# Attention steps issued singly and in 64-column pieces, turning joined with later scores, and a plan that counts instruction blocks

## The chip, the cores and the metric

The kernel runs on one core of one Trainium2 chip. The metric is the device time of one execution in microseconds, lower is better. Three runs of the kernel before took 547.86, 543.38 and 552.81 us; their median, 547.86 us, is the time before. The tensor engine is called PE here, its weight loads PEld, the vector engine DVE, the scalar engine ACT, GpSimd POOL and the engine that issues the transfers SP.

## What is computed

A recurrent attention (mLSTM) over 4 batches, 8 heads, 768 positions and head size 40, followed by a feed-forward part of 320 to 2048 to 320 on the 3072 tokens that come out. All in float32.

```python
for t in range(S):
    m_new = np.maximum(f_gate[:, :, t] + m, i_gate[:, :, t])
    f_stab = np.exp(f_gate[:, :, t] + m - m_new)
    i_stab = np.exp(i_gate[:, :, t] - m_new)
    m = m_new
    C = f_stab[..., None, None] * C + i_stab[..., None, None] * np.einsum('bhd,bhe->bhde', vt, kt)
    n = f_stab[:, :, None] * n + i_stab[:, :, None] * kt
    h_tilde = np.einsum('bhde,bhe->bhd', C, qt)
    denom = np.maximum(np.abs(np.einsum('bhd,bhd->bh', n, qt)[:, :, None]), 1.0)
    y[:, :, t] = h_tilde / (1.0 + np.exp(-o_gate[:, :, t])) / denom
...
h = x @ w_in                                   # x: y of all heads, 3072 x 320
sp = np.maximum(h, 0.0) + np.log1p(np.exp(-np.abs(h)))
out = (h * erf(sp)) @ w_out
```

## The kernel before

The sequence is cut into 6 chunks of 128 positions (`NC`, `L`). Within a chunk the recurrence becomes matrix products with a decay mask; between chunks a state of 40 x 41 per head is carried, kept in `state[b]` for each batch. A step of attention is one chunk and two batches, `attention(c, bs)`, so there are 12 steps. Each step gives 256 tokens, and the feed-forward part works on them in four groups, `mlp(g)`, of 512 of the 2048 hidden columns each: 48 groups in all.

For each batch of a step, in this order:

- SP loads q and k (`qk`, 416 KB, line 413) and k, v and the output gate (`kvo`, 484 KB, line 417), and from the second chunk on the spread gates (`dm` and `eT`, lines 437 to 445).
- `dm` becomes the decay mask: DVE adds (line 449), ACT takes the exponential (453), POOL cuts the triangle (459). DVE makes `vg`, v times the gates (469).
- `scores` (line 472) multiplies k and q on PE: 16 calls with 64 columns of weights each, 128 columns streamed.
- DVE multiplies scores and mask (525) and scales q (531).
- `heads` (line 482) does three products on PE. q times the state (491) and masked scores times v (495) are cut into four pieces of 32 rows of output, called quarters. k times `vg`, the addition to the state, is cut into 32 and 8 rows (503), and left out in the last chunk. Each call streams 41 columns.
- DVE divides and applies the output gate (559 to 575) into the output part of `kvo`, and renews the state (580 to 585).
- `turned` (506) transposes y on PE in three calls of 128 x 128 (509). ACT rounds it to the high half `xh` (600), DVE takes the rest as the low half `xl` (604). `mlp` reads these.

In `mlp`, two products of 16 calls each fill `h` (729); ACT copies it (737) and applies softplus and erf (741, 745), with table loads between kinds of function; DVE multiplies and splits (749 to 759); PE multiplies with the output weights (779 for the first 8 groups, 781 to 784 after). The weights of the feed-forward part are loaded and decoded at the start by `weights_in`, `weights_tail` and `weights_out`, and split by `split_out`.

The order of all this is made by a planner in the kernel itself. Every piece of work is handed to `Plan.add` by `op` with its engine, an assumed cost, what it reads and writes, and the buffers that it takes; `run` then simulates the five engines and always starts the ready operation with the earliest due time. Due times come from hand-set numbers (`STEPS` for attention steps, `FIRST_DUE`, `EVERY` and `LAG` for the groups, `WIN` and `WOUT` for weights) and are passed back from later operations to earlier ones in `dues`. On PE an operation of the same kind as the last one is preferred:

```python
due = o.due - (1.0 if e == 'PE' and o.kind == mode else 0.0)
```

The resulting order is fixed in the program; on the chip each engine runs its own list and waits on semaphores. Where the plan shows PE idle for over 0.9 us, filler matmuls (`stay`, line 826) are put in. Buffers are limited by `SLOTS`: 3 each of `qk`, `kvo` and `dm`, 2 each of `xh` and `xl`, two double PSUM banks `pa` and two of `h`; several share a pool of 23. From the third chunk on (`BUNDLE`), the scores of both batches are one operation of the plan, and so are both `heads` and both `turned`.

Of the kernel before, what the change touches and what calls it, by code (L numbers as in the profile page):

```python
# [18 lines left out]
L = 128  # L19
# [14 lines left out]
class Plan:  # L34
# [5 lines left out]
    GAP, FILL = 0.9, 0.6  # L40
    RATE = 240e3
    INORDER = ('qk', 'kvo', 'dm', 'eT', 'vg', 'xh', 'xl', 'x', 'aT')

    def __init__(self, slots, shared=(), total=0):
        self.slots, self.shared, self.total = dict(slots), shared, total
        self.ops, self.wrote, self.read = [], {}, {}
        self.users, self.tag = {}, {}
        self.kinds = []
        self.queue = {}

# [4 lines left out]
    def add(self, eng, cost, fn, r=(), w=(), new=(), phase=None, due=None, kind=None, name=None, after=(), sets=None):  # L55
        i = len(self.ops)
        o = SimpleNamespace(i=i, eng=eng, cost=cost, fn=fn, phase=phase, kind=kind, name=name, sets=sets,
                            due=1e9 if due is None else due, deps=set(), succ=[], new=[], tiles=set())
# [49 lines left out]

    def run(self, switch, stay=None):
        self.dues()  # L110
        n = len(self.ops)
        left = [len(o.deps) for o in self.ops]
        ready = [0.0] * n
# [21 lines left out]
        while count < n:  # L135
# [21 lines left out]
            for e in ('PE', 'DVE', 'ACT', 'POOL', 'SP'):  # L157
# [19 lines left out]
                for o in cand[e]:  # L177
# [6 lines left out]
                    if any(slots[self.tag[k]] < sum(self.tag[x] == self.tag[k] for x in o.new)  # L184
                           or self.tag[k] in self.INORDER and self.queue[self.tag[k]][0] != k for k in o.new):
                        continue
                    due = o.due - (1.0 if e == 'PE' and o.kind == mode else 0.0)
# [6 lines left out]
                for k in o.new:  # L194
                    slots[self.tag[k]] -= 1
                    total -= self.tag[k] in self.shared
                    if self.tag[k] in self.INORDER:
                        self.queue[self.tag[k]].pop(0)
# [36 lines left out]
FIRST_DUE = [23.7, 87.5, 23.0, 49.5, 86.4, 67.7, 62.7, 193.4]  # L235
EVERY = 4.25
WIN = [1.8, 14.7, 24.1, 45.9, 2.3, 9.1]
WOUT = [26.4, 28.5, 69.5, 41.6]
# [12 lines left out]
def tile_mlstm_moe(  # L251
# [15 lines left out]
    plan = Plan(SLOTS, WIDE, WIDES)  # L267
    t = {}
# [75 lines left out]
    def gate_chunk(c):  # L344
        @dma(128, w=[(('gt', c), 0)], tile_=('gt', ('gt', c)))
# [51 lines left out]
    def attention(c, bs):  # L397
# [12 lines left out]
        for b in bs:  # L410
# [9 lines left out]
            if c == 0:  # L420
                @op('PE', 3.8, r=[(('x', c), 0), ('ident', 0)], w=[K('pb', b)], tile_=('pa', ('pb', c, b)), kind='a')
# [60 lines left out]
        def heads(b):  # L482
            p_ = new('pa', [128, 1024], ('ph', c, b)).rearrange("p (j w) -> p j w", j=2)
            y = p_[:, :, 0:NPR * V1].rearrange("p j (n d) -> p j n d", d=V1)
            quarters = [slice(32 * i, 32 * i + 32) for i in range(4)]
            q, w, v, st = A('qk', b)[:, 0], dm(b), v1(b), state[b]
            for p in range(NPR if c > 0 else 0):
                for ts in quarters:
# [3 lines left out]
            for p in range(NPR):  # L492
                for j in range(2):
                    for ts in quarters:
                        nc.tensor.matmul(y[ts, j, p], w[:, j, p, ts], v[:, 2 * p + j], start=(c == 0),  # L495
                                         stop=(c == 0 or p == NPR - 1))
            if not last:
                pk = p_[:, 0, NPR * V1:2 * NPR * V1].rearrange("p (n d) -> p n d", d=V1)
                k, vg = kn(b), A('vg', b)
                for p in range(NPR):  # L500
                    for d in (slice(0, 32), slice(32, D)):
                        for j in range(2):
                            nc.tensor.matmul(pk[64 * j + d.start:64 * j + d.stop, p], k[:, 2 * p + j, d], vg[:, 2 * p + j],  # L503
                                             start=True, stop=True)

        def turned(b):
            p = new('pa', [128, 1024], ('pt', c, b))
            for i in range(3):
                nc.tensor.transpose(p[:, i * L:(i + 1) * L], A('kvo', b)[:, KV + i * 128:KV + (i + 1) * 128], ident)  # L509

        def bundles():
            return [[b] for b in bs] if c < BUNDLE else [list(bs)]

        for bb in bundles():
            @op('PE', 1.05 * len(bb), r=[K('qk', b, n) for b in bb for n in 'qk'], w=[K('S', b) for b in bb],
                tile_=[('pa', ('S', c, b)) for b in bb], kind='a',
                after=[K('dm', b) for b in bb] + ([] if last else [K('vg', b) for b in bb]))
            def _(bb=bb):
                for b in bb:
                    scores(b)  # L520
# [12 lines left out]
        for bb in bundles():  # L533
            @op('PE', (0.57 + (0.35 if c else 0) + (0 if last else 0.33)) * len(bb),
                r=[k for b in bb for k in [K('dm', b), K('kvo', b, 'v'), K('kvo', b, 'k')] + ([] if last else [K('vg', b)])
                   + ([K('qk', b, 'q'), ('st', b)] if c else [])],
                w=[K('ph', b) for b in bb], kind='a',
                tile_=[('pa', ('ph', c, b)) for b in bb] + ([('xh', ('xh', hc)), ('xl', ('xl', hc))] if bb[0] == bs[0] else []))
            def _(bb=bb):
                if bb[0] == bs[0]:  # L540
                    for n in ('xh', 'xl'):
                        new(n, [128, 3, T], (n, hc), F32R)
                for b in bb:
                    heads(b)
# [42 lines left out]
        for bb in bundles():  # L587
            @op('PE', 0.35 * len(bb), r=[K('kvo', b, 'o') for b in bb] + [('ident', 0)], w=[K('pt', b) for b in bb],
                tile_=[('pa', ('pt', c, b)) for b in bb], kind='a')
            def _(bb=bb):  # L590
                for b in bb:
                    turned(b)

        for b in bs:
            ts = slice(b % 2 * L, (b % 2 + 1) * L)
            pt = lambda b=b: A('pt', b)[:, 0:3 * L].rearrange("p (n t) -> p n t", t=L)

            @op('ACT', 0.45, r=[K('pt', b)], w=[(('xh', hc), b % 2)])
            def _(b=b, ts=ts, pt=pt):
                nc.scalar.activation(t['xh', hc][:, :, ts], pt(), AF.Copy)  # L600

            @op('DVE', 0.53, r=[K('pt', b), (('xh', hc), b % 2)], w=[(('xl', hc), b % 2)])
            def _(b=b, ts=ts, pt=pt):
                nc.vector.tensor_tensor(t['xl', hc][:, :, ts], pt(), t['xh', hc].bitcast(F32)[:, :, ts], op=ALU.subtract)  # L604

# [35 lines left out]
    def weights_in(part, k):  # L641
        R = ('raw', part, k)
# [10 lines left out]
    def weights_tail(i):  # L653
        R, HL = ('rawt', i), ('hl', i)
# [25 lines left out]
    def weights_out(j):  # L680
        R, W = ('rawo', j), ('wo', j)
# [11 lines left out]
    def split_out(j):  # L693
        W, N = ('wo', j), ('wol', j)
# [10 lines left out]
    def mlp(g):  # L705
        k, q = divmod(g, 4) if g >= 8 else (g % 2, g // 2)
# [8 lines left out]
        for i in range(2):  # L715
            @op('PE', 1.9, r=[((n, k), b) for n in ('xh', 'xl') for b in range(2)]
# [44 lines left out]
        for b in range(2):  # L761
            for lo in (None,) if plain else range(2):
# [7 lines left out]
                @op('PE', 2.2 if plain else 0.59 * (2 - lo), r=reads, w=[(key, b)], tile_=tile_, kind='m',  # L770
# [25 lines left out]
    gate_chunk(0)  # L796
    for i in range(2):
        step_due[0] = STEPS[i]
        attention(0, (2 * i, 2 * i + 1))
    step_due[0] = None  # L800
    for part in range(4):
        step_due[0] = WIN[part]
        for k in range(2):
            weights_in(part, k)
        if part % 2 == 0:
            step_due[0] = WIN[4 + part // 2]
            weights_tail(part // 2)
        step_due[0] = WOUT[part]
        for j in range(4):
            weights_out(4 * part + j)  # L810
    step_due[0] = None
    for g in range(8):
        mlp(g)
    for j in range(NFF):
        split_out(j)
    for c in range(1, NC):
        gate_chunk(c)
        for i in range(2):
            step_due[0] = STEPS[2 * c + i]
            attention(c, (2 * i, 2 * i + 1))  # L820
        step_due[0] = None
        for g in range(8 * c, 8 * c + 8):
            mlp(g)
# [69 lines left out]
```

## Time and profile before

| | |
|---|---|
| median of three runs | 547.86 us (543.38 to 552.81) |
| the profiled execution | 549.43 us |
| its span, first to last instruction | 547.7 us |
| mean granted clock of PE | 0.933 |
| matmuls and weight loads on PE | 7117 and 7117 |
| DMA moved | 54.31 MB, mean 99 GB/s |

The profile is of one execution. A row of the table of engines has the busy time, its share of the span and the number of instructions. A row of the queues has packets, megabytes and the share of the DMA engines' time. "Issue" is the time in which an engine stood without waiting for anything that the profile shows. In the timeline a row has its start, its length, engine, line, operation, tiles, shape and count, and in brackets the idle time before it and what ended that. In a table by stretch, each engine has its busy time and in brackets its instructions, in the order PE, PEld, DVE, ACT, POOL (or PE alone), then the granted clock of PE (1.00 is full), the share of the DMA engines and GB/s. In the chain, a row has its start, its length, and the engine, tile, line and count. In the table of waits, a row has who waited for whom, the total in us, the number of times and the longest.

### The profile page before, as it was taken

To read this page: it belongs to the slowest core of one execution; us is meant where nothing else is said; L and a number is where in the kernel's file an instruction comes from. 1 tells how busy PE (TensorE), PEld (TensorE's weight loads), DVE (VectorE), ACT (ScalarE), POOL (GpSimd) and SP (SyncE) were. 2 spreads that over 40 slices of the span, in tenths; PEclk is the share of its full clock that TensorE was granted. 3 is DMA by queue.
4 is the path that set the end of the run, shared out by engine and by line. 5 is a ranking of instruction groups with operands and counts; after the bars stand their busy time and mean duration, and the time that the engine had idled before them with its cause. 6 is when DMAs were issued, how large, how long until landed. Compare 5 with 4: busy or idle time off the path is not lost.

```text
span 547.7 us, 15952 instructions
## 1 busy us (share of the span) xinstructions
PE 489.6 (89%) x7117; PEld 462.2 (84%) x7117; DVE 338.1 (62%) x599; ACT 312.5 (57%) x419; POOL 41.8 (8%) x60
## 2 busy tenths in 40 slices
PE   8978899698997989889959978995999699989996
PEld 8867888567986979789949977995899699989996
DVE  3869899587795758477529376641654525473362
ACT  3537999543692867428835740366177148546563
POOL 2300021000001001002002020000010000000000
PEclk9979999989897989979969996998799979999999
DMA  8965993432426423432124041305300400000000
GB/s 234 234 180 194 306 308 93 121 102 84 131 92 160 159 72 105 127 105 68 36 77 136 24 105 53 117 13 153 105 1 25 139 1 26 1 28 1 1 24 25
DMA packets 28180, 54.31 MB, mean 99 GB/s; under 512 B 2896, under 2 KB 16144, under 8 KB 28112
## 3 DMA queue, kind: packets, MB, share of 16 engines
q1 hardware_dynamic: 28112, 53.30, 33.1%
q8 instruction: 56, 0.92, 0.7%
q14 instruction: 12, 0.10, 0.1%
HBM read 48.14 MB, written 4.10 MB: 95 GB/s over the span
## 4 chain that ended last, share of the span: by engine, by line
PE 85%; issue 9%; ACT 3%; DVE 2%; POOL 0%; ACTq 0%; POOLq 0%
PE h L729 33%; PE pob L783 9%; PE pob L784 9%; PE pob L781 9%; PE pa L495 4%; PE pa L479 4%; PE pob L779 3%; PE pa L779 3%; PE pa L491 3%; PE pa L503 2%; PE pa L509 2%; PE pob L826 1%; PE pa L427 1%; PE pa L428 1%; ACT L828 1%
## 5 line engine op out<-in xcount | busy, mean ns | idle before, releaser
L729 PE MATMUL h<-xh,wh 128*128 128x256 f32 x576 | 163.2, 292 | 1.7 <-ACT hb L737 1.7
L729 PE MATMUL h<-xl,wh 128*128 128x256 f32 x576 | 160.1, 287 | 0.0
L737 ACT ACTIVATE hb<-h 128x512 f32<-128x512 f32 x96 | 56.4, 596 | 135.6 <-PE h L729 134.4
L729 PEld LDWEIGHTS h<-xh,wh 128*128 128x128 f32 x576 | 111.7, 194 | 9.1 <-issue 6.4
L729 PEld LDWEIGHTS h<-xl,wh 128*128 128x128 f32 x576 | 111.6, 194 | 0.4 <-DVE xl L604 0.2
L729 PE MATMUL h<-xh,wl 128*128 128x256 f32 x384 | 110.2, 287 | 0.0
L783 PE MATMUL pob<-woh,gh 128*128 128x320 f32 x320 | 101.4, 327 | 1.3 <-ACT o L789 1.1
L784 PE MATMUL pob<-wo,gh 128*128 128x320 f32 x320 | 99.1, 321 | 0.0
L749 DVE TENSOR_TENSOR n<-n,hb 128x1024 f32<-128x1024 f32 x48 | 59.1, 1239 | 63.2 <-ACT n L745 63.1
L828 ACT ACT_TABLE_LOAD x61 | 78.3, 1283 | 1.8 <-PEq L881 0.8
L729 PEld LDWEIGHTS h<-xh,wl 128*128 128x128 f32 x384 | 74.5, 194 | 0.0
L459 POOL TENSOR_SCALAR_AFFINE_SELECT dm<-dm 128x512 f32<-128x512 f32 x48 | 40.3, 863 | 406.9 <-ACT dm L453 305.7
L783 PEld LDWEIGHTS pob<-woh,gh 128*128 128x128 f32 x320 | 63.9, 200 | 3.1 <-ACT o L789 1.6
L784 PEld LDWEIGHTS pob<-wo,gh 128*128 128x128 f32 x320 | 64.0, 200 | 0.1
L781 PE MATMUL pob<-woh,gl 128*128 128x320 f32 x320 | 61.0, 318 | 0.0
L741 ACT ACTIVATE n<-hb 128x1024 f32<-128x1024 f32 x48 | 50.6, 1060 | 5.5 <-PE pa L491 4.3
L781 PEld LDWEIGHTS pob<-woh,gl 128*128 128x128 f32 x320 | 51.1, 195 | 0.4 <-issue 0.2
L759 DVE TENSOR_TENSOR gl<-n,gh 128x1024 fp32r<-128x1024 f32 x40 | 49.7, 1243 | 1.6
L559 DVE COPY den<-pa 128x8 f32<-128x8 f32 x24 | 4.0, 165 | 73.7 <-PE pa L503 61.0
L745 ACT ACTIVATE n<-n 128x1024 f32<-128x1024 f32 x48 | 48.6, 1052 | 0.2
L495 PE MATMUL pa<-kvo,dm 128*32 128x41 f32 x1536 | 23.8, 219 | 16.6 <-issue 16.6
L495 PEld LDWEIGHTS pa<-kvo,dm 128*32 128x32 f32 x1536 | 20.0, 123 | 21.3 <-issue 20.1
(73 smaller groups left out, 587.5 us busy)
## 6 DMA issues: line engine op xcount, KB each, us to landing
kvo<-in_kvo_dram SPq DMA_DIRECT2D x24, 484.0 KB
dm<-gd SPq DMA_DIRECT2D x20, 512.0 KB
qk<-in_qk_dram SPq DMA_DIRECT2D x24, 416.0 KB
raw<-in_w_out_dram SPq DMA_DIRECT2D x16, 320.0 KB
raw<-in_w_in_dram SPq DMA_DIRECT2D x8, 512.0 KB
out_dram<-o SPq DMA_DIRECT2D x24, 160.0 KB
eT<-gd SPq DMA_DIRECT2D x20, 128.0 KB
eT<-gd SPq DMA_DIRECT2D x20, 80.0 KB
```

Of the source, the lines that this page charges most:

```text
L459: nc.gpsimd.affine_select(out=x, in_=x, pattern=[[0, 4], [1, L]], compare_op=ALU.is_ge, fill=0.0, base=0, channel_multiplier=-1)
L495: nc.tensor.matmul(y[ts, j, p], w[:, j, p, ts], v[:, 2 * p + j], start=(c == 0), stop=(c == 0 or p == NPR - 1))
L729: nc.tensor.matmul(h[:, n * T:(n + 1) * T], w, m, start=(s == 0), stop=(s == len(ops) - 1))
L737: nc.scalar.activation(G('hb')[:, hs], G(f'h{i}'), AF.Copy)
L741: nc.scalar.activation(new('n0', [128, 1024], ('n0', g)), G('hb'), AF.Softplus)
L745: nc.scalar.activation(G('n0'), G('n0'), AF.Erf)
L749: nc.vector.tensor_tensor(G('n0'), G('n0'), G('hb'), op=ALU.mult)
L759: nc.vector.tensor_tensor(new('gl', [128, 1024], ('gl', g), F32R), G('n0'), G('gh').bitcast(F32), op=ALU.subtract)
L781: nc.tensor.matmul(acc(b), G('gl')[:, ts], woh[:, j], start=False, stop=(j == NFF - 1))
L783: nc.tensor.matmul(acc(b), G('gh')[:, ts], woh[:, j], start=(j == 0), stop=False)
L784: nc.tensor.matmul(acc(b), G('gh')[:, ts], t['wol', j], start=False, stop=False)
L828: order = plan.run(lambda k: nc.scalar.preload_act_table_set(KIND[k]), stay)
```

## The change

There are four parts.

- `heads` cuts its products into two pieces of 64 rows where it had four of 32, and k times `vg` into one piece of 40 rows where it had 32 and 8.
- `BUNDLE` is gone: scores, `heads` and turning of each batch are operations of their own in every chunk.
- For the first three steps (`JOIN = 3`) y is turned within its own step, by `finish`. From the fourth on, the turning of batch i of a step is put at the head of the operation with the scores of batch i of the next step, and the division into halves follows there; the last step's is done at the end. The order in which steps and groups are handed to the planner is changed to fit.
- The planner counts PE's matmuls (`mm`) in blocks of 126 and assumes that a block takes at least 6.5 us from its start until the next can start (`fetch`). When it chooses for PE, eight times the delay that an operation would have by this is added to its due time. Each operation also belongs to a part (a step, a group, a weight tile) and an engine, and a table `SHIFT` of 348 numbers from -349.0 to 281.6 us is added to the due times by part and engine. The hand-set due times and several assumed costs have new values. The filler matmuls are counted by 0.25 or 0.45 us each where it was 0.23.

```diff
+    BLOCK, FETCH, SPREAD, SAME = 126, 6.5, 8.0, 1.0
...
+    def fetch(self, now, cost, mm):
+
+        at, begun = self.block
+        while at + mm >= self.BLOCK:
+            n = self.BLOCK - at
+            now = max(now + cost * n / mm, begun + self.FETCH)
+            cost, mm, at, begun = cost * (mm - n) / mm, mm - n, 0, now
+            if not mm:
+                break
+        return now + cost, (at + mm, begun)
...
+        for o in self.ops:
+            o.due = o.due0 + self.shift.get(o.part, 0.0)
...
-                    due = o.due - (1.0 if e == 'PE' and o.kind == mode else 0.0)
+                    due = o.due
+                    if e == 'PE':
+                        due += self.SPREAD * (self.fetch(now, o.cost, o.mm)[0] - now - o.cost) - self.SAME * (o.kind == mode)
...
+                    end, self.block = self.fetch(now, cost, o.mm)
+                    cost = end - now
...
-                    n = int((o.start - last.end) * self.FILL / 0.23)
+                    n = int((o.start - last.end) * self.FILL / (0.25 if last.end > 9 else 0.45))
...
-FIRST_DUE = [23.7, 87.5, 23.0, 49.5, 86.4, 67.7, 62.7, 193.4]
-EVERY = 4.25
...
-LAG = 8.77
-STEPS = [5.5, 23.6, 67.5, 123.9, 137.6, 149.5, 198.2, 250.9, 271.9, 280.0, 320.6, 344.3]
+FIRST_DUE = [58.8, 85.9, 31.4, 64.5, 93.1, 98.3, 67.5, 208.5]
+EVERY = 4.63
...
+LAG = 3.83
+STEPS = [4.2, 25.0, 70.7, 132.0, 151.6, 158.4, 209.1, 256.1, 285.7, 291.2, 340.6, 352.6]
...
-BUNDLE, PLAIN = 2, 8
+PLAIN, JOIN = 8, 3
...
+    def turned(c, b):
+        p = new('pa', [128, 1024], ('pt', c, b))
+        for i in range(3):
+            nc.tensor.transpose(p[:, i * L:(i + 1) * L], t['kvo', c, b][:, KV + i * 128:KV + (i + 1) * 128], ident)
+
+    def divided(c, bs):
+        hc = 2 * c + bs[0] // 2
+        for b in bs:
+            ts = slice(b % 2 * L, (b % 2 + 1) * L)
+            pt = lambda b=b: t['pt', c, b][:, 0:3 * L].rearrange("p (n t) -> p n t", t=L)
+
+            @op('ACT', 0.45, r=[(('pt', c, b), 0)], w=[(('xh', hc), b % 2)])
...
+            @op('DVE', 0.53, r=[(('pt', c, b), 0), (('xh', hc), b % 2)], w=[(('xl', hc), b % 2)])
...
+    def finish(c, bs):
+        for b in bs:
+            @op('PE', 0.35, r=turned_from(c, b), w=turned_to(c, b), tile_=('pa', ('pt', c, b)), kind='a', mm=6)
+            def _(b=b):
+                turned(c, b)
+
+        divided(c, bs)
...
-            quarters = [slice(32 * i, 32 * i + 32) for i in range(4)]
+            sides = [slice(64 * i, 64 * i + 64) for i in range(2)]
...
-                    for d in (slice(0, 32), slice(32, D)):
-                        for j in range(2):
-                            nc.tensor.matmul(pk[64 * j + d.start:64 * j + d.stop, p], k[:, 2 * p + j, d], vg[:, 2 * p + j],
-                                             start=True, stop=True)
...
+                    for j in range(2):
+                        nc.tensor.matmul(pk[64 * j:64 * j + D, p], k[:, 2 * p + j], vg[:, 2 * p + j], start=True, stop=True)
+
+        for i, b in enumerate(bs):
+            was = (prev[0], prev[1][i]) if prev else ()
+
+            @op('PE', 1.05 + (0.35 if prev else 0), r=[K('qk', b, n) for n in 'qk'] + turned_from(*was), w=[K('S', b)] + turned_to(*was),
+                tile_=[('pa', ('S', c, b))] + [('pa', x[0]) for x in turned_to(*was)], kind='a', mm=38 if prev else 32,
+                after=[K('dm', b)] + ([] if last else [K('vg', b)]))
+            def _(b=b, was=was):
+                if was:
+                    turned(*was)
+                scores(b)
+
+        if prev:
+            divided(*prev)
...
+        for b in bs:
+            @op('PE', 0.68 + (0.45 if c else 0) + (0 if last else 0.35), mm=32 + (32 if c else 0) + (0 if last else 16),
...
+    pairs = [(c, (2 * i, 2 * i + 1)) for c in range(NC) for i in range(2)]
+    prev = None
+    for k, (c, bs) in enumerate(pairs):
+        if k % 2 == 0:
+            gate_chunk(c)
+        step_due[0] = STEPS[k]
+        attention(c, bs, prev)
+        step_due[0] = None
+        if prev:
+            for g in range(4 * k - 4, 4 * k):
+                mlp(g)
+        prev = None
+        if k < JOIN:
+            step_due[0] = STEPS[k]
+            finish(c, bs)
...
+        else:
+            prev = c, bs
```

More of the change, by code (lines that the diff above doesn't have):

```diff
@@ L49, in __init__ @@
         self.queue = {}
+        self.part, self.shift = None, {}
     def phase(self, kind):
@@ L53, in phase, with add @@
         return len(self.kinds) - 1
-    def add(self, eng, cost, fn, r=(), w=(), new=(), phase=None, due=None, kind=None, name=None, after=(), sets=None):
+    def add(self, eng, cost, fn, r=(), w=(), new=(), phase=None, due=None, kind=None, name=None, after=(), sets=None, mm=8):
         i = len(self.ops)
-        o = SimpleNamespace(i=i, eng=eng, cost=cost, fn=fn, phase=phase, kind=kind, name=name, sets=sets,
+        o = SimpleNamespace(i=i, eng=eng, cost=cost, fn=fn, phase=phase, kind=kind, name=name, sets=sets, mm=mm, part=self.part and self.part + ':' + eng,
                             due=1e9 if due is None else due, deps=set(), succ=[], new=[], tiles=set())
@@ L107, in dues @@
                 last = min([o.due for o in mine], default=last)
-    def run(self, switch, stay=None):
-        self.dues()
+    def fetch(self, now, cost, mm):
[7 more added lines that the diff above has]
+        return now + cost, (at + mm, begun)
+    def run(self, switch, stay=None):
+        queue = {k: list(v) for k, v in self.queue.items()}
+        if not hasattr(self.ops[0], 'due0'):
+            self.dues()
+            for o in self.ops:
+                o.due0 = o.due
+        for o in self.ops:
+            o.due = o.due0 + self.shift.get(o.part, 0.0)
         n = len(self.ops)
         left = [len(o.deps) for o in self.ops]
+        self.block = 0, -10.0
         ready = [0.0] * n
@@ L267, in tile_mlstm_moe @@
     plan = Plan(SLOTS, WIDE, WIDES)
+    plan.shift = SHIFT
     t = {}
@@ L344, in gate_chunk @@
     def gate_chunk(c):
+        plan.part = f'g{c}'
         @dma(128, w=[(('gt', c), 0)], tile_=('gt', ('gt', c)))
@@ L394, in _, with turned_from, turned_to, attention @@
                 nc.sync.dma_start(t['gd', c][:, b].rearrange("i h t -> h i t"), t['x', c][32 * b:32 * b + H, 1:3])
-    def attention(c, bs):
+    def turned_from(*step):
+        return [(('kvo', *step), 'o'), ('ident', 0)] if step else []
+    def turned_to(*step):
+        return [(('pt', *step), 0)] if step else []
+    def turned(c, b):
[8 more added lines that the diff above has]
+            @op('ACT', 0.45, r=[(('pt', c, b), 0)], w=[(('xh', hc), b % 2)])
+            def _(b=b, ts=ts, pt=pt):
+                nc.scalar.activation(t['xh', hc][:, :, ts], pt(), AF.Copy)
+            @op('DVE', 0.53, r=[(('pt', c, b), 0), (('xh', hc), b % 2)], w=[(('xl', hc), b % 2)])
+            def _(b=b, ts=ts, pt=pt):
+                nc.vector.tensor_tensor(t['xl', hc][:, :, ts], pt(), t['xh', hc].bitcast(F32)[:, :, ts], op=ALU.subtract)
+    def finish(c, bs):
[4 more added lines that the diff above has]
+        divided(c, bs)
+    def attention(c, bs, prev=None):
+        plan.part = f'a{c}{bs[0]}'
         last = c == NC - 1
@@ L531, in _ @@
                     nc.vector.tensor_tensor(q, q, A('eT', b)[0:QR], op=ALU.mult)
[L533 to L540, printed above, removed]
+        for b in bs:
+            @op('PE', 0.68 + (0.45 if c else 0) + (0 if last else 0.35), mm=32 + (32 if c else 0) + (0 if last else 16),
+                r=[K('dm', b), K('kvo', b, 'v'), K('kvo', b, 'k')] + ([] if last else [K('vg', b)])
+                + ([K('qk', b, 'q'), ('st', b)] if c else []), w=[K('ph', b)], kind='a',
+                tile_=[('pa', ('ph', c, b))] + ([('xh', ('xh', hc)), ('xl', ('xl', hc))] if b == bs[0] else []))
+            def _(b=b):
+                if b == bs[0]:
                     for n in ('xh', 'xl'):
                         new(n, [128, 3, T], (n, hc), F32R)
[L543 to L544 removed]
+                heads(b)
         for b in bs:
@@ L641, in weights_in @@
     def weights_in(part, k):
+        plan.part = f'i{part}{k}'
         R = ('raw', part, k)
@@ L653, in weights_tail @@
     def weights_tail(i):
+        plan.part = f't{i}'
         R, HL = ('rawt', i), ('hl', i)
@@ L680, in weights_out @@
     def weights_out(j):
+        plan.part = f'o{j}'
         R, W = ('rawo', j), ('wo', j)
@@ L693, in split_out @@
     def split_out(j):
+        plan.part = f's{j}'
         W, N = ('wo', j), ('wol', j)
@@ L705, in mlp @@
     def mlp(g):
+        plan.part = f'm{g}'
         k, q = divmod(g, 4) if g >= 8 else (g % 2, g // 2)
@@ L794, in _ @@
                     nc.sync.dma_start(out[r:r + L, :], t['o', k, b])
[L796 to L812, printed above, removed]
-        mlp(g)
[L814 to L823, printed above, removed]
+    pairs = [(c, (2 * i, 2 * i + 1)) for c in range(NC) for i in range(2)]
[13 more added lines that the diff above has]
+            finish(c, bs)
+            step_due[0] = None
+            if k > 1:
+                for g in range(4 * k, 4 * k + 4):
+                    mlp(g)
+        else:
+            prev = c, bs
+        if k == 1:
+            for part in range(4):
+                step_due[0] = WIN[part]
+                for n in range(2):
+                    weights_in(part, n)
+                if part % 2 == 0:
+                    step_due[0] = WIN[4 + part // 2]
+                    weights_tail(part // 2)
+                step_due[0] = WOUT[part]
+                for j in range(4):
+                    weights_out(4 * part + j)
+            step_due[0] = None
+            for g in range(8):
+                mlp(g)
+            for j in range(NFF):
+                split_out(j)
+    finish(*prev)
+    for g in range(4 * len(pairs) - 4, 4 * len(pairs)):
+        mlp(g)
     def stay(n):
```

47 lines of the change are left out of this document (10 added, 37 removed).

## The prediction

> **What bounds the kernel now.** I read the page first, then the core's clock, the table of waits, the timeline of TensorE (PE) around its longest pauses, and tables by stretch.
>
> ```profile
> PE 489.6 (89%) x7117; PEld 462.2 (84%) x7117; DVE 338.1 (62%) x599; ACT 312.5 (57%) x419; POOL 41.8 (8%) x60
> q8 instruction: 56, 0.92, 0.7%
> PE 85%; issue 9%; ACT 3%; DVE 2%; POOL 0%; ACTq 0%; POOLq 0%
> ```
> ```profile
> core 0: 547.7 us, clock 0.933
> ```
> ```profile
> PE pa L491 <- issue: 18.6, 5, 6.3
> PE pa L495 <- issue: 16.6, 7, 5.0
> PE pa L503 <- issue: 12.4, 7, 2.5
> PE h L729 <- ACT hb L737: 1.7, 1, 1.7
> ```
>
> PE is the chain (85%). What is not PE is "issue": PE stands still with no producer late. Waits of PE on another engine are small, the largest 1.7 us. The three issue rows sum to 18.6 + 16.6 + 12.4 = 47.6 us, and all three lines are the small matmuls of `heads`. Why there? The timeline of one pair of batches:
>
> ```profile
> 373.20 0.78 PE L491 MATMUL pa<-state,qk 40*32 40x41 f32 x64
> 373.92 0.82 PE L495 MATMUL pa<-kvo,dm 128*32 128x41 f32 x64
> 374.54 0.49 PE L503 MATMUL pa<-vg,kvo 128*32 128x41 f32 x32
> 374.96 0.27 PE L491 MATMUL pa<-state,qk 40*32 40x41 f32 x5
> 381.57 0.91 PE L491 MATMUL pa<-state,qk 40*32 40x41 f32 x59 [6.34 <-issue]
> 385.14 0.72 PE L503 MATMUL pa<-vg,kvo 128*8 128x41 f32 x28 [1.28 <-issue]
> ```
> ```profile
> 280.14:328.18 48.04, 43.72 (x637) 0.93 0.26 73
> 328.18:381.56 53.38, 44.50 (x637) 0.88 0.31 88
> 381.56:438.47 56.91, 50.61 (x763) 0.92 0.22 66
> 438.47:491.20 52.73, 50.85 (x637) 0.95 0.04 14
> ```
>
> The pause falls inside a run of one line, after 5 of 64 matmuls, so it is no dependence and no change of shape. The second fence cuts the span at the ends of five such pauses and counts PE's matmuls between them: 637, 637, 763, 637, that is 5, 5, 6 and 5 times 127.3. Each matmul has its weight load (x7117 both), so pauses sit on multiples of about 255 instructions. Queue q8 moved 0.92 MB of instructions in 56 packets, and 7117 / 127.3 = 55.9. So PE's program comes in blocks of about 127 matmuls, and PE pauses where it uses a block up before the next is there. One `heads` of a batch issues 160 matmuls in 374.96 - 373.20 = 1.76 us (11.0 ns each): more than a block. Two ends of pauses stand 385.14 - 381.57 = 3.57 us apart; the block before them took about 8 us (373.5 to 381.57). A block therefore needs 3.6 to 8 us.
>
> [...]
>
> The pauses cost a second time, through the clock:
>
> ```profile
> 163.74:167.40 3.66, 1.60 (x140) 1.35 (x130) 2.38 (x7) 2.09 (x5) 2.07 (x2) 1.00 0.13 24
> 167.50:174.20 6.70, 4.60 (x96) 4.30 (x83) 2.77 (x11) 0.00 (x0) 0.00 (x0) 0.50 0.95 246
> 381.57:388.80 7.23, 5.95 (x166) 5.55 (x167) 2.73 (x11) 0.00 (x0) 0.43 (x1) 0.50 0.03 9
> 445.00:453.00 8.00, 8.00 (x61) 7.99 (x60) 0.00 (x0) 6.44 (x7) 1.22 (x2) 1.00 0.01 2
> ```
>
> The column after POOL is the granted clock. Right after the 6.34 us pause it is 0.50 for 7.2 us; in undisturbed stretches 1.00. Over the core 0.933 means (1 - 0.933) x 547.7 = 36.7 us of full clock not granted. In 381.57:388.80 PE was busy 5.95 of 7.23 us (82%), so about 30 us of the 36.7 fell on work.
>
> **The change part by part.** The sum goes against the profiled execution: its own time 549.4 us, its span 547.7, the median of the runs shown 547.9, so the sum is 1.5 us above that median.
>
> 1. Fewer instructions. `heads` uses 64-column pieces for the state product, the score product, and k times v. Per batch of a middle chunk that is 64 + 64 + 32 = 160 matmul records before and 32 + 32 + 16 = 80 after (all these operations are recorded twice per call). The program falls by 640 + 768 + 320 = 1728 of 7117 matmuls, to about 42 blocks. The price of one 64-column matmul of 41 streamed columns is in no row. Lower bound: the 11.0 ns pace above, 80 x 11.0 = 0.88 us per batch. Upper bound: the scores, which are 64 columns wide but stream 128:
>
> ```profile
> 156.52 1.91 PE pa L479 x64
> 180.46 0.66 PE pa L509 x6
> 215.87 3.83 PE h L729 x32
> 214.70 1.17 PE pob L781 x8
> ```
>
> 1.91 / 64 = 29.8 ns, 80 x 29.8 = 2.39 us. I take 17.5 ns, 1.40 us, nearer the lower end because the streamed 41 columns are those of the row that gives it. Against 1.76 us that saves 0.36 x 16 batches of the four middle chunks = 6 us. Ends: (1.76 - 0.88) x 16 = 14 us saved to (2.39 - 1.76) x 16 = 10 us lost.
>
> 2. The plan knows of blocks, and batches run singly. Before, from chunk 2 on both batches' `heads` stand in one operation: 320 matmuls, 2.5 blocks in 3.5 us, against 3.6 to 8 us per block. After, one `heads` is 80 matmuls; filled up to 127 with 47 matmuls of the MLP (3.83 / 32 = 0.12 us each, 5.6 us) the block lasts 7.0 us. That covers the short need and leaves at most 1 us of the long. Where scores and turning (35 records) and `heads` (80) meet in one block it lasts 0.96 + 0.33 + 1.40 + 12 x 0.12 = 4.1 us (turning at 0.66 / 6 = 0.11 us per transpose), and 0 to 3.9 us are open. There is material enough: a pair of batches now has 2 x 115 = 230 attention matmuls beside 4 x 56 = 224 of the MLP. I leave about 1 us for each of the 10 pairs after chunk 0: 10 us of 47.6 stay, 37.6 go. Ends: 2 to 30 us stay. The plan's count is not the chip's (126 against 127.3 per block, 6 against 3 records for a turning), so its boundaries drift by up to half a block; that is why I do not take zero.
>
> 3. The clock. If pauses shrink to 10 / 47.6 = 21%, 30 x 0.21 = 6 us of loss remain; I keep 9, since two pauses of about 2 us were enough for the 0.50 at 167.50. That saves 21 us. [...]
>
> ```profile
> 166.12 0.39 PE L503 MATMUL pa<-vg,kvo 128*8 128x41 f32 x18 [2.06 <-issue]
> 170.05 0.55 PE L495 MATMUL pa<-kvo,dm 128*32 128x41 f32 x18 [2.10 <-issue]
> ```
>
> 4. Turning joined with later scores. Eight times (steps 4 to 11) the three transposes of the step before are issued with the next scores. Their own time moves, it does not grow. New: MLP groups of a step can start only when the next step's scores do, which need its mask times gates (`dm`, over SP, DVE, ACT and POOL) and `vg`; and a step's `kvo` stays held, so with three slots the load for the second batch waits on SP for a turning, with the loads for `dm`, `eT` and the outputs behind it. The cover is the four MLP groups of the step before: 4 x (3.83 + 3 x 1.17) = 29 us. The load is 484 KB, 2 us at the 246 GB/s of the row at 167.50. SP already stands long for outputs without holding PE:
>
> ```profile
> SPq L794 <- ACT o L789: 213.2, 16, 36.6
> ```
>
> I put 3 us for new waits; ends 0 and 30.
>
> 5. The start. Part of the pauses lies before 108 us, where the other engines are nearly full:
>
> ```profile
> 26.76 3.66 issue
> 98.59 1.93 issue
> 105.21 3.00 issue
> ```
> ```profile
> 63.40:108.20 44.80, 39.37 (x526) 32.76 (x527) 37.26 (x74) 38.66 (x64) 6.72 (x8) 1.00 0.67 187
> 108.20:540.00 431.80, 392.31 (x5728) 375.27 (x5727) 253.80 (x423) 238.13 (x298) 27.70 (x33) 0.92 0.25 72
> ```
>
> ACT is busy 38.66 of 44.80 us there (86%), so of these 8.6 us I count 5 as given back to ACT. From 108 us on DVE has 253.8 and ACT 238.1 of 431.8 us; if that stretch shrinks by 55 us, DVE is at 67%: late next would be no engine as a whole, only single hand-overs of `h` to ACT.
>
> New dues, the `SHIFT` table, the changed count of filler matmuls and the fetch term in `run` add no instruction of weight; what they do is the order, costed in 2 and 4.
>
> Sum: 549.4 - 6 - 37.6 - 21 + 3 + 5 = 492.8, so **493 us**. With the ends that go with working blocks (heads 14 saved, 4 us of pauses, no new waits) it comes to about 474; with heads 10 lost or 10 us of new waits to 512.
>
> **The rivals.**
>
> A. The blocks stay short half the time. For it: the long pauses stand where data move (the fetch of 8 us), the plan assumes 6.5 us always, and its boundaries drift. Against it: 24% fewer blocks in any case. Half of both losses kept: 549.4 - 6 - 24 - 15 + 8 = 512, with a quarter of the gain about 532.
>
> B. The join starves PE, the one that ends slower. If `dm` or `vg` of the next step comes later than the 29 us of MLP cover, PE stands at each of the eight joins. It passes 549.4 x 1.02 = 560 us when each costs (560 - 493) / 8 = 8.4 us or more, say 570. Against it: PE's waits on other engines are 1.7 us at most now, and DVE and ACT have a third or more free.
>
> C. The change doesn't do what it says: pauses are not the blocks, or are paid back elsewhere (drains between shapes, hidden fetch), and only the 64-column pieces count, 549.4 - 6 + 8 = 551, so 538 to 560. Against it: the multiples of 127.3 and the pause after 5 of 64 equal matmuls.
>
> **How the numbers follow.** Forecast (474 to 512) 0.64, A (512 to 532) 0.16, C 0.09, B 0.07, and 0.04 for under 474, where the start gains too. Within 2% (537 to 559), about what a measurement of this kernel can tell from no change, is C: 0.10 with the slow end of A. Faster 0.83, slower 0.07. The range is 474 to 532, which leaves out 0.20; the forecast's own is 474 to 512.
>
> **What would show it.** Right: q8 near 42 packets, matmuls near 5400, issue rows of PE under 15 us together, clock 0.97 or more, `heads` of a middle batch near 1.4 us from first to last. Wrong: issue rows over 25 us (A); PE rows that name DVE, ACT or DMA at the scores line with tens of us (B); pauses that no longer come at multiples of a block (C). The forecast fails if PE's waits move from issue to `h` or `dm`, or if the first 108 us grow.

## The result: 509 us, and the profile after

The changed kernel takes 509.17 us (median of four runs, 507.83 to 510.40) against 550.34 us before; the ratio is 0.933, 95% interval 0.925 to 0.942. The ratio leaves out the two of the four runs before that lie over 1.5% above the fastest (552.81 and 557.06 us), so it stands a little higher than 509.17 / 550.34 = 0.925. The profiled execution took 507.83 us, its span is 506.1 us. The forecast was 493 us with a range of 474 to 532.

The page of the changed kernel, in the rows that answer to those shown before:

```profile
PE 483.3 (95%) x5405; PEld 451.7 (89%) x5405; DVE 344.6 (68%) x599; ACT 313.8 (62%) x419; POOL 44.1 (9%) x60
q8 instruction: 42, 0.69, 0.6%
PE 73%; DVE 10%; ACT 9%; DMA 5%; issue 2%; SPq 1%; ACTq 0%; DVEq 0%
```
```profile
core 0: 506.1 us, clock 0.988
```

PE has 5405 matmuls where it had 7117, and q8 brought 42 blocks where it brought 56 (5405 / 127.3 = 42.5). The clock is nearly full: (1 - 0.988) x 506.1 = 6.1 us of full clock not granted, against 36.7. But PE is busy 483.3 us, only 6 us less than before, and DVE (10%), ACT (9%) and DMA (5%) have a larger part of the chain, where DVE and ACT had 5% together. The table of waits of PE, its first five rows:

```profile
PE pa L434 <- DVE kvo L630: 2.8, 3, 1.5
PE pob L823 <- ACT o L831: 2.6, 5, 0.5
PE pob L825 <- ACT o L831: 2.3, 4, 0.7
PE h L771 <- ACT hb L779: 2.1, 3, 0.9
PE pa L553 <- DVE m L383: 2.1, 1, 2.1
```

No row of PE's table says "issue" any more: all 47.6 us of pauses are gone. In their place stand many small waits, mostly for DVE and ACT. The chain shows a late start:

```profile
8.28 11.23 DMA kvo<-in_kvo_dram
19.52 6.11 DMA qk<-in_qk_dram
25.63 0.14 issue
25.77 1.10 PE pa L541 x32
```

The first scores wait for q and k until 25.8 us; before, they started at 18.1 us (the row gives the shortest, median and longest length in ns, then first and last start):

```profile
L479 PE MATMUL pa<-qk x768: 269/269/473, 18.1 to 480.2; 40*64 40x128 f32 x192
```

And one `heads` in the timeline, now in 64-column pieces:

```profile
298.32 0.68 PE L553 MATMUL pa<-state,qk 40*64 40x41 f32 x32
298.92 1.13 PE L557 MATMUL pa<-kvo,dm 128*64 128x41 f32 x32
299.88 0.49 PE L564 MATMUL pa<-vg,kvo 128*40 128x41 f32 x16
300.29 0.85 PE L823 MATMUL pob<-woh,gl 128*128 128x320 f32 x4
```

From start to start the three products take 0.60, 0.96 and 0.41 us, 1.97 us in all against 1.76 before. Half the instructions did not save PE time: masked scores times v has 0.96 / 32 = 30 ns a record, while its 32-column pieces, in the timeline shown in the prediction, took (374.54 - 373.92) / 64 = 9.7 ns (11.0 ns was the mean over all three products).

### The profile page after: what moved, and what is told of

It reads as the page before. It is cut to its first block, busy times and chain, and to the rows that moved or that the text cites. A ratio compares the mean times of both kernels' runs of the same rounds, so it can differ in the third digit from the quotient of the medians.

```text
span 506.1 us, 12514 instructions
## 1 busy us (share of the span) xinstructions
PE 483.3 (95%) x5405; PEld 451.7 (89%) x5405; DVE 344.6 (68%) x599; ACT 313.8 (62%) x419; POOL 44.1 (9%) x60
## 4 chain that ended last, share of the span: by engine, by line
PE 73%; DVE 10%; ACT 9%; DMA 5%; issue 2%; SPq 1%; ACTq 0%; DVEq 0%
PE h L771 30%; PE pob L825 9%; PE pob L823 8%; PE pob L826 8%; PE pa L541 4%; PE pa L557 4%; PE pa L821 3%; PE pob L821 3%; ACT L882 2%; DMA kvo<-in_kvo_dram 2%; PE pa L553 2%; ACT n L787 2%; ACT n L783 1%; DVE n L791 1%; ACT hb L779 1%
## 5 line engine op out<-in xcount | busy, mean ns | idle before, releaser
L771 PE MATMUL h<-xh,wh 128*128 128x256 f32 x576 | 158.5, 286 | 2.1 <-ACT hb L779 2.1
L771 PE MATMUL h<-xl,wh 128*128 128x256 f32 x576 | 156.3, 282 | 0.8 <-DVE xl L448 0.8
L771 PEld LDWEIGHTS h<-xh,wh 128*128 128x128 f32 x576 | 108.4, 188 | 4.5 <-ACT hb L779 3.0
L825 PE MATMUL pob<-woh,gh 128*128 128x320 f32 x320 | 97.1, 315 | 2.7 <-ACT o L831 2.3
L826 PE MATMUL pob<-wo,gh 128*128 128x320 f32 x320 | 95.1, 309 | 0.0
L825 PEld LDWEIGHTS pob<-woh,gh 128*128 128x128 f32 x320 | 60.1, 188 | 5.9 <-ACT o L831 3.3
L826 PEld LDWEIGHTS pob<-wo,gh 128*128 128x128 f32 x320 | 60.2, 188 | 0.0
L583 DVE TENSOR_TENSOR dm<-pa,dm 128x1024 f32<-128x1024 f32 x24 | 29.4, 1223 | 32.0 <-PE pa L541 31.7
L515 ACT ACTIVATE dm<-dm 128x1024 f32<-128x1024 f32 x20 | 20.9, 1058 | 26.2 <-DVE dm L511 26.1
L797 DVE CAST gh<-n 128x1024 fp32r<-128x1024 f32 x40 | 28.8, 719 | 0.7
```

What stands on the lines that cost most here:

```text
L771: nc.tensor.matmul(h[:, n * T:(n + 1) * T], w, m, start=(s == 0), stop=(s == len(ops) - 1))
L825: nc.tensor.matmul(acc(b), G('gh')[:, ts], woh[:, j], start=(j == 0), stop=False)
L826: nc.tensor.matmul(acc(b), G('gh')[:, ts], t['wol', j], start=False, stop=False)
```

## The experiments

The theory to test was the forecast's: PE's program comes in blocks of about 127 matmuls, and fewer and better spread attention matmuls end the pauses and the half clock. The rivals were that the order alone does it, and that the pauses are something else. Later runs ask what the new order costs. Every time is a median of four runs, every ratio goes against the kernel before on the same chip. On the four chips of the experiments the kernel before took 549.67 to 551.29 us, so times from different chips can be compared to within about 2 us.

### Pieces without the order, and the order without the pieces

First run: the kernel before with its order untouched, and 64-column pieces.

```diff
-            quarters = [slice(32 * i, 32 * i + 32) for i in range(4)]
+            sides = [slice(64 * i, 64 * i + 64) for i in range(2)]
...
-                    for d in (slice(0, 32), slice(32, D)):
-                        for j in range(2):
-                            nc.tensor.matmul(pk[64 * j + d.start:64 * j + d.stop, p], k[:, 2 * p + j, d], vg[:, 2 * p + j],
-                                             start=True, stop=True)
+                    for j in range(2):
+                        nc.tensor.matmul(pk[64 * j:64 * j + D, p], k[:, 2 * p + j], vg[:, 2 * p + j], start=True, stop=True)
```

> The kernel before with its order untouched; only heads issues 64-column pieces (80 matmul records for a batch of a middle chunk instead of 160). Block theory: the two heads of a bundle are 160 records in about 3.9 us instead of 320 in 3.5 us, so one boundary falls into a bundle instead of two or three; PE's issue rows fall from 47.6 us to 15 to 25 us, the clock rises from 0.933 to about 0.965, the heads cost 5 to 8 us more work: 515 to 528 us, q8 near 42 packets. Rival 1 (pauses are drains between tile shapes, or come with the order alone): issue rows stay near 45 us and the time near 550 us or above. Rival 2 (the pieces are the whole change): issue rows under 5 us and 505 to 512 us.

Measured: 492.07 us, ratio 0.896 (0.891 to 0.901), faster than the whole change and below every time that I had expected. The page and the waits of this kernel:

```profile
PE 471.6 (96%) x5389; PEld 446.9 (91%) x5389; DVE 342.1 (70%) x599; ACT 312.7 (64%) x419; POOL 43.8 (9%) x60
q8 instruction: 42, 0.69, 0.6%
```
```profile
PE pa L502 <- issue: 2.5, 1, 2.5
...
PE pob L781 <- issue: 1.5, 1, 1.5
```

The largest issue rows are 2.5 and 1.5 us (all four together 5.5 us), the clock 0.995. I had expected 15 to 25 us of pauses to stay. Two `heads` of 80 records are 160 in 2 x 1.97 = 3.9 us, so a block of 127 is used up in about 3.1 us, less than the 3.6 to 8 us that the forecast gave a block, and yet there is next to no pause. So that need was put too high, or more than one block was ready; which of the two was not tried. The pieces halve the number of instructions and also double the time from one to the next (11.0 ns before, 1.97 / 80 = 24.6 ns in the changed kernel), and no run holds one of these still. The pieces alone bring more than the whole change does.

Second run: the changed kernel with its order, and the pieces of 32 columns put back (the diff above, reversed).

> The changed kernel with its order untouched; only heads is cut into 32-column pieces again (160 records for a batch), while the plan goes on counting 80. Block theory: heads of one batch is longer than a block of 127, so a second boundary falls into it in about a quarter of cases and close behind it in others; pauses of 2 to 6 us return, 15 to 30 us of issue rows in all, clock 0.95 to 0.97, less 7 us of heads work: 520 to 545 us, q8 near 55 packets. Rival (the new order alone removed the pauses): no issue rows, heads cheaper by 7 us, about 500 us.

Measured: 534.84 us, ratio 0.973 (0.967 to 0.979), 56 blocks again, clock 0.974.

```profile
PE pa L565 <- issue: 11.8, 6, 2.4
PE pa L557 <- issue: 11.7, 5, 3.2
```

The pauses are back with the instructions, 23.5 us in these rows. They still stand on blocks. Cut just ahead of the ends of successive long pauses, the trace has these counts of PE's matmuls:

```profile
141.22:172.86 31.64, 28.33 (x510) 0.95 0.28 87
172.86:213.57 40.71, 38.45 (x637) 1.00 0.38 112
213.57:237.27 23.70, 21.32 (x382) 1.00 0.39 108
279.13:324.89 45.76, 42.18 (x765) 0.96 0.33 95
```

510, 637, 382 and 765 are 4, 5, 3 and 6 times 127.3 to within 2 matmuls, in a program whose order is another than that of the kernel before. With the old pieces the new order halves the pauses (47.6 to 23.5 us). What in the order does it was not tried apart; the next run speaks only for the new pieces. With these there is next to nothing left to remove, and the order costs 17 us (509.2 against 492.1).

### The block term in the plan's choice

```diff
-    BLOCK, FETCH, SPREAD, SAME = 126, 6.5, 8.0, 1.0
+    BLOCK, FETCH, SPREAD, SAME = 126, 6.5, 0.0, 1.0
```

> The changed kernel with SPREAD 0: the plan still simulates the block waits but its choice on PE takes no account of them, so the order is another. If the spreading in the plan is needed: scores and heads meet in one block, 8 to 20 us of issue rows on PE return and the clock falls to 0.97 or below: 518 to 530 us. If pieces and single batches suffice: issue rows under 5 us and 506 to 512 us. A time above 535 us would say that the order itself got worse for another reason (waits on DVE, ACT or DMA), to be read from the table of waits.

Measured: 509.01 us, ratio 0.927 (0.921 to 0.934), and no issue row in PE's table. Choosing by blocks made no difference that can be measured: with 80 records to a `heads`, issued one batch at a time, no pause came that it could have avoided.

### Which width for masked scores times v

Since the 64-column piece of this product is dearer, it went back to 32 columns in three orders: that of the changed kernel, that of the kernel before, and that of a run below (`e7_old_numbers`).

```diff
+            quarters = [slice(32 * i, 32 * i + 32) for i in range(4)]
...
-                    for ts in sides:
+                    for ts in quarters:
                         nc.tensor.matmul(y[ts, j, p], w[:, j, p, ts], v[:, 2 * p + j], start=(c == 0),
```

> The changed kernel with its order untouched; only masked scores times v is cut into 32-column pieces again (64 records of about 11 ns instead of 32 of about 31 ns); the state product and k times vg stay at 64. heads is 112 records, still under a block. If the width of the pieces, not the order, made this product dearer: it falls from about 1.0 to 0.7 us per batch, 24 batches, 7 us less PE work; if blocks still stay covered 500 to 504 us, with some pauses back 504 to 510. Rival (the cost comes from batches issued singly, with a change of shape at each end): the product stays near 1.0 us and the time at 508 to 512.

Measured: 509.07 us, ratio 0.927 (0.922 to 0.932): no change, though the product is cheaper. The group of this product, in the changed kernel and then in this run:

```profile
L557 PE MATMUL pa<-kvo,dm 128*64 128x41 f32 x768 | 28.0, 234 | 0.7 <-ACT dm L494 0.7
```
```profile
L558 PE MATMUL pa<-kvo,dm 128*32 128x41 f32 x1536 | 20.1, 205 | 0.0
```

28.0 us of busy time became 20.1, so the width makes the price, not the order. From start to start one such product takes 0.74 us here against 0.96 us, about 5 us over 24 batches. The gain went elsewhere; a pause of 2.8 us is back, the wait for q and k is 3.6 us long (1.7 in the changed kernel), and the clock is 0.983 (0.988). Whether these are the whole of it was not tried.

```profile
PE pa L541 <- DMA qk<-in_qk_dram: 3.6, 1, 3.6
PE h L772 <- issue: 2.8, 1, 2.8
```

> e1_pieces_only with masked scores times v cut into 32 columns again; order as in the kernel before. A batch's heads is 112 records, a bundle of two 224 in about 3.3 us, 1.8 blocks, where e1_pieces_only has 160 in 3.9 us. Block theory: the product gets 5 us cheaper (e4_y_in_quarters showed 5.5 us of PE work) but a second boundary falls into most bundles, 10 to 20 us of issue rows and some half clock come back: 497 to 515 us. Rival (the blocks are no limit once heads is under 127 records): no issue rows, 486 to 489 us.

Measured: 510.65 us, ratio 0.924 (0.919 to 0.929), 18.6 us slower than the first run, with 48 blocks and clock 0.970.

```profile
PE pa L496 <- issue: 14.4, 5, 5.7
PE pa L503 <- issue: 3.7, 1, 3.7
```

Two `heads` of 112 records side by side are 224 in 2 x 1.79 = 3.6 us, and 18.1 us of pauses are back in these rows, as the block theory said. The wide piece costs PE more and is right here all the same: it is one instruction for two, and 160 in 3.9 us went nearly without pauses.

> e7_old_numbers with the same product in 32 columns; heads of single batches stand apart, 112 records each, so blocks should stay covered: the 5 us of PE work become 4 to 6 us of time, 493 to 496 us. If the saved work is lost again in waits or in the start, as in e4_y_in_quarters: 498 to 502 us.

Measured: 506.70 us, ratio 0.919 (0.915 to 0.924), 7 us slower than the same order with the wide piece, where I expected 4 to 6 us less. It has 3.4 us of issue in one row, and a clock of 0.980 (0.997 with the wide piece) means (0.997 - 0.980) x 505.7 = 8.6 us more of full clock not granted. Less the 5 us saved on the product, these come to about the 7 us, by estimate. The expectation fell: 112 records in single batches are not covered everywhere.

### What the new order costs

The first run again, with scores, `heads` and turning of each batch apart in all chunks, under the old planner:

```diff
-BUNDLE, PLAIN = 2, 8
+BUNDLE, PLAIN = 6, 8
```

> e1_pieces_only with BUNDLE 6: scores, heads and turning of each batch are operations of their own in every chunk, under the old planner with its old numbers; no join, no block term, no SHIFT. If issuing batches singly is what the new order loses (a change of shape at both ends of twice as many operations): transposes, scores and heads take 5 to 10 us more PE work than in e1_pieces_only and the time is 497 to 503 us. If singles are free or help the blocks: 488 to 494 us, and issue rows below the 5 us of e1_pieces_only.

Measured: 497.62 us, ratio 0.905 (0.899 to 0.911), 5.5 us above the first run. The two intervals overlap by a little, so the size is less sure than the sign. PE is busy 474.7 us against 471.6, so about 3 us of it are longer work of PE.

Then the changed kernel with the old hand-set numbers and without `SHIFT`, once without joins and once with them:

```diff
-    plan.shift = SHIFT
...
-PLAIN, JOIN = 8, 3
+PLAIN, JOIN = 8, 12
```

> The changed kernel without joins (JOIN 12), without SHIFT and with the hand-set due times of the kernel before; block term and new costs stay. With e7_old_numbers it shows the join alone. If the new numbers and SHIFT are the loss: 488 to 497 us. If the block term or the new costs are: 500 to 510 us.

> The changed kernel, joins included, without SHIFT and with the hand-set due times of the kernel before. If the joins starve PE: over 3 us slower than e6_no_join_old_numbers, with PE rows that wait for DVE, ACT or DMA at the scores line. If they are free: within 2 us of it. If the new numbers with SHIFT are what loses against e1_pieces_only, mostly by the later start: 488 to 498 us, first scores before 20 us.

Measured: 498.74 us without joins, ratio 0.906 (0.900 to 0.911); 499.76 us with them, ratio 0.908 (0.903 to 0.913). Both lie just under 2 us above the range expected if the new numbers and `SHIFT` were the loss. With the old numbers the eight joins cost about 1 us, which these runs can't tell from nothing, and no row of PE's waits at the scores line shows PE starved.

Then the changed kernel without `SHIFT` alone, with its new hand-set numbers:

```diff
-    plan.shift = SHIFT
```

> The changed kernel without the SHIFT table alone; its new hand-set numbers stay. It lies between the changed kernel (509 us) and e7_old_numbers (500 us, which has the old hand-set numbers too). If SHIFT is the loss: 498 to 502 us. If the new hand-set numbers are, chosen to go with SHIFT: 507 us or more.

Measured: 493.84 us, ratio 0.895 (0.891 to 0.900). I expected 498 us or more; the table of 348 numbers costs 509.17 - 493.84 = 15.3 us, nearly all that stands between the change and the forecast. The new hand-set numbers are better than the old ones without it (493.8 against 499.8 us).

Two runs look for the place. One brings the first q and k forward in the changed kernel, the other puts the `SHIFT` numbers of the start alone into the run without `SHIFT`:

```diff
-SHIFT = {..., 'a00:SP': 2.5, ...}
+SHIFT = {..., 'a00:SP': -60.0, ...}
```

> The changed kernel with one number altered: the SHIFT of the first step's loads is -60 instead of 2.5, so kvo and q and k of the first two batches are issued ahead of most weight loads (as in the kernel before). Later order changes with it. If the start is what costs: first scores at 17 to 20 us instead of 25.8, and 5 to 9 us less in all, 500 to 504 us. If the weights then come later and take the gain back: 506 to 512 us, with the first h matmuls no earlier.

Measured: 530.36 us, ratio 0.963 (0.957 to 0.969): worse by 21 us and outside both expectations. The first scores did start at 18.6 us, but a part of the input weights came later (its first copy into `wh` is issued at 41.6 us, in the changed kernel at 25.3), and the first `h` product began at 52.1 us where the changed kernel has it at 40.8:

```profile
L541 PE MATMUL pa<-qk x768: 269/269/472, 18.6 to 442.7; 40*64 40x128 f32 x192
```
```profile
L771 PE MATMUL h<-xh,wh x576: 276/281/561, 52.1 to 506.1; 128*128 128x256 f32 x192
```
```profile
L771 PE MATMUL h<-xh,wh x576: 278/281/522, 40.8 to 483.6; 128*128 128x256 f32 x192
```
```profile
L825 PE MATMUL pob<-woh,gh x320: 304/309/421, 178.2 to 523.0; 128*128 128x320 f32 x160
```

(The third row is of the changed kernel; the rows give first and last start.) The last row, of this run, is a later product of the feed-forward part, which starts at 156.0 us in the changed kernel and there has its last start at 500.6 us: 22.2 us are lost by then, and 22.4 at the end. One number moved the whole start, so the run says nothing of early q and k by themselves; early q and k did not make an early start. It shows how much a start weighs. PE also has 5.0 us in two issue rows here, at counts that are not those of block ends.

> e11_no_shift (494 us) with the SHIFT numbers back for the first gates, the two steps of the first chunk and the input weights alone, so that most input weights are issued ahead of the first kvo and q and k, as in the changed kernel; the later parts have no SHIFT. If the late start is the larger part of what SHIFT costs: first scores at 22 to 27 us instead of 18.8, and 499 to 504 us. If the loss lies in the later parts: 492 to 496 us in spite of late first scores.

Measured: 502.88 us, ratio 0.917 (0.913 to 0.922), 9.0 us above the run without `SHIFT` and inside what was expected of a late start, with the first scores at 24.2 us where that run has them at 18.8. First and last start of a product of the feed-forward part, without `SHIFT`, with it at the start, and in the changed kernel:

```profile
L824 PE MATMUL pob<-woh,gh x320: 304/309/421, 144.5 to 486.2; 128*128 128x320 f32 x160
```
```profile
L825 PE MATMUL pob<-woh,gh x320: 303/309/421, 153.2 to 495.1; 128*128 128x320 f32 x160
```
```profile
L825 PE MATMUL pob<-woh,gh x320: 303/309/421, 156.0 to 500.6; 128*128 128x320 f32 x160
```

With `SHIFT` at the start alone the product begins 153.2 - 144.5 = 8.7 us later and ends 8.9 us later: what is lost by then never comes back. In the changed kernel it is 11.5 us at the first and 14.4 us at the last. So most of the loss is made before 156 us, and about 3 us after. In the tables it hardly shows as waits of PE, because the plan puts filler matmuls into the gaps that it foresees, and they count as busy. The fillers without `SHIFT`, with it at the start, and in the changed kernel:

```profile
L879 PE MATMUL pob<-ident 128*128 128x128 f32 x46 | 7.5, 315 | 0.0
```
```profile
L880 PE MATMUL pob<-ident 128*128 128x128 f32 x112 | 16.6, 300 | 0.0
```
```profile
L880 PE MATMUL pob<-ident 128*128 128x128 f32 x78 | 12.8, 322 | 0.0
```

With `SHIFT` at the start they are 16.6 - 7.5 = 9.1 us more, as much as the span grew (500.6 - 491.8 = 8.8 us); in the changed kernel 5.3 us more, of 14.3 us. Whether the fillers only fill the wait or hold other work back was not tried. That the late q and k are the cause within the start was not shown: the run moves weights, gates and attention together.

## Why the forecast was right in sign and 16 us short

**The pauses** (part 2 of the forecast, 10 us to stay). The first two runs show that pauses and blocks go with the pieces in the old order (47.6 us and 56 blocks to 5.5 us and 42), and come back with them in the new one (23.5 us and 56), again at multiples of 127.3. That PE stands there because the next block is not yet at hand is my reading of these counts. The size was too careful: no issue row stayed. The reason given, batches issued apart by a plan that counts blocks, was not needed; 80 records instead of 160 did it. In the changed kernel the ends of its 42 blocks cost no pause that the table of waits shows; with the old pieces in the same order there are 56 blocks and 23.5 us of pauses.

**The clock** (9 us to stay). 6.1 us were not granted in the changed kernel. The clock rose where pauses went, 0.995 with the pieces alone, and fell where they returned, 0.974 and 0.970. What is left in the changed kernel stands mostly behind other waits: the half clock stands behind the wait for q and k (1.7 us in the table of waits) and behind the 2.1 us for DVE there:

```profile
26.77:30.18 3.41, 3.41 (x34) 0.50 0.98 252
108.69:115.52 6.83, 6.83 (x87) 0.50 0.17 43
```

The forecast read the 0.50 at 167.50 as the work of two pauses of about 2 us. The second began at 170.05 - 2.10 = 167.95 us, after the clock had fallen (at 167.47 us), so one had been enough for it to fall.

**The 64-column pieces** (6 us saved). Wrong in sign: 1.97 instead of 1.76 us a batch, (1.97 - 1.76) x 16 = 3.4 us lost, inside the bounds of 14 saved to 10 lost. I took a value near the row of the same 41 columns; for masked scores times v the other end was right, 30 ns against the 29.8 ns of the scores, though it streams a third of their columns. The size shows in the run with this product in 32 columns, which took back about 5 us of PE's work.

**The joins** (in the 3 us for new waits). About 1 us, not told from nothing; the rival that they starve PE fell.

**The order** is the step that failed. The forecast said that new dues and `SHIFT` "add no instruction of weight; what they do is the order, costed in 2 and 4", 3 us. `SHIFT` costs 15.3 us; without it the changed kernel takes 493.8 us, the time that was forecast. That it comes so near is partly luck, because the errors have opposite signs: pauses and clock were put 10 + 3 us too high, the pieces 6 + 3.4 us too low. That 509 lies inside the forecast's own 474 to 512 is in part luck too: the upper end was made of dear pieces or new waits, not of a late start. That end does not follow from the sum either, in which 10 us lost on `heads` give 508.8, 10 us of new waits 499.8, and both 515.8. The start was counted as 5 us given back from a gain, not as a loss of its own: the forecast did not ask when the first loads would come, and the diff showed only numbers from which that could not be read. It had named the sign, though ("if the first 108 us grow"): the product that first starts at 156.0 us in the changed kernel starts at 153.0 us in the kernel before, where 8.6 us of pauses and more stand ahead of it, and at 141.5 us with the pieces alone. What in the late start costs the time, loads, gates or fillers, stays open.

**The rivals.** A stands closest in time (512 to 532) but not in kind, since the blocks did not stay short. B fell with the joins, and C with the pauses that stood on blocks and went with the pieces; the drains between shapes and the hidden fetch that C named as ways to pay them back were guesses that no run shows. The kernel before with the pieces alone (492.1 us) and the changed kernel without `SHIFT` (493.8 us) beat both kernels; the two do not differ by what these runs can tell.

## What to carry to other kernels

Where PE pauses for "issue" inside a run of equal small matmuls, count matmuls between the pauses; if the counts are multiples of one number, as here of 127.3, look to the stream of instructions, and try fewer, larger instructions even where each costs more. Test the smallest part of such a change alone first: here a few lines did more than all of it. And when a change replaces an order, ask when the first work that needs all its inputs can begin: here PE was busy nearly to the end, and what the start lost was still missing at the last product.

## What the runs showed that I had not expected

A 64-column piece of masked scores times v takes as long as about three 32-column ones (30 ns a record against 9.7 in the kernel before and 0.74 / 64 = 11.6 in the run with this product in 32 columns), so per column it is dearer; k times `vg` with 40 columns takes 0.41 us for 16 records (26 ns), against 0.42 us for 32 records of 32 and 8 columns. And one pause of about 2.5 us did not always halve the clock: the pieces alone have one of 2.5 us at 253.87 us and no half clock behind it, while the kernel before fell to 0.50 after one of 2.06 us. The rows are the timeline and a table by stretch of the pieces alone, with PE's busy time, count and granted clock.

```profile
253.87 0.39 PE L502 MATMUL pa<-vg,kvo 128*40 128x41 f32 x10 [2.46 <-issue]
```
```profile
254.00:264.00 10.00, 10.00 (x85) 1.00 0.39 105
```

Where a pause lies may make the difference. In the trace of the kernel before, all 24 records of the granted clock begin a whole number of 3.41 us after the first, which begins at 7.05 us; so do all 6 in the trace of the changed kernel, where the first begins at 9.70 us. Here are stretches of that length and of twice it, first of the kernel before, from an edge of this grid on, then of the pieces alone, where I read the grid from 6.63 us on:

```profile
164.06:167.47 3.41, 1.35 (x114) 1.00 0.12 20
167.47:174.30 6.83, 4.73 (x99) 0.50 0.95 245
```
```profile
248.98:252.39 3.41, 2.42 (x98) 1.00 0.95 256
252.39:255.80 3.41, 1.93 (x21) 1.00 0.05 18
```

The pause of 2.06 us falls whole into one stretch, and the next has half the clock. The pause of 2.46 us is split, 0.98 us in one stretch and 1.48 us in the next, and neither is followed by half the clock. In the traces of the kernel before and of the changed kernel, cut so, a stretch of 3.41 us at full clock with 1.8 us or more of PE idle was followed by 0.50 in 11 of 11 cases, one with less than 1 us in none of 258; between these it went either way (2 of 8). That this sharing out is the cause is my estimate from these counts; no run moved a pause along the grid to test it.
